# Gate rows through DRAM, join sums moved, weight loads reordered: one change to a fused spectral-filter and gated-MLP kernel

## Chip, cores, metric

One core of one Trainium2 chip. The metric is the device time of one execution in microseconds (us). A timed kernel is run several times, in turn with the kernel before on the same chip. A ratio is the mean time of one kernel's fast runs over the mean of the fast runs of the other in the same rounds, so it is not quite the ratio of the medians that are quoted. Faster or slower means by more than 2%. A profile is of one execution, taken by the hardware profiler: one of the timed ones, but for the kernel before, whose profile is of a further execution of 250.93 us. Its span is 1.7 to 2.0 us shorter than the timed figure of the same execution, so spans are compared with spans and medians with medians. Runs are marked slow (over 1.5% above the fastest of the same kernel); they stand in no ratio.

## The reference

```python
mod = (_silu(c) @ w_mod).reshape(1, 6, 1, 640)       # c: 1 x 640, w_mod: 640 x 3840
sa, ca, ga, sb, cb, gb = ...                         # six rows of 640
h = _layernorm(x) * (1 + ca) + sa                    # x: 1 x 2048 x 640
x = x + ga * irfft2(rfft2(h) * (w_r + 1j * w_i))     # spectral filter
h = _layernorm(x) * (1 + cb) + sb
x = x + gb * ((silu(h @ w_gate) * (h @ w_up)) @ w_down)   # w_gate: 640 x 1728
```

All tensors are bf16. Six modulation vectors are needed. `ca`, `sa`, `cb`, `sb` are used as columns (one value per partition). `ga` and `gb` are used as rows, the same row on all 128 partitions: `ga` multiplies the table `RI` of the last transform, `gb` multiplies the down weights.

## The kernel before, where the change touches it

The kernel runs in stages. **Stage 1** (to 35.8 us) makes layer norm 1 and the forward transform over the 640 columns. The **middle stage** takes spectral columns in groups: TensorE transforms a group (`stage_a`), VectorE multiplies by the filter (`prod`, two products per group, over the filter `Wn` and its flipped copy `Wv`), TensorE transforms back (`stage_b`, `stage_c`), and VectorE or GpSimd fill in the rotated halves (`rot`). At the **changeover** the first tiles of the last transform start (`s1em`, `s1er`). The **last spectral stage** makes 16 tiles of x1; layer norm 2 (LN2) of its first tiles, with a DMA transpose, is made beside it. Then come the **gate/up** and down products, continuous TensorE work to the end.

`Wn` and `Wv` each have three planes: real, imaginary and a "join sum" of both, made in pieces by `wsum` on VectorE or GpSimd.

```python
# SyncE's queue, early: gate-a weights (800 KB) ahead of Wv
nc.sync.dma_start(wm_r[:, :, 0, :], wm_m[:, :, 0, :])
nc.sync.dma_start(KS2, K_dram[:, 384:576])
# ... (cut)
for i in range(2):
    nc.sync.dma_start(Wv[:, 2 * i, :, :], Wflip[i][:])
# ... stage 1 (cut); then four DMA transposes in a row, and what follows them
t2_dma(0); t2_dma(1); t2_dma(2); t2_dma(3)
nc.sync.dma_start(wm_r[:, :, 1:3, :], wm_m[:, :, 1:3, :])   # LN2's weights, 1600 KB
nc.sync.dma_start(wm_r[:, :, 3, :], wm_m[:, :, 3, :])       # gate-b weights, 800 KB
nc.sync.dma_start(Htab[:], H_dram)
nc.sync.dma_start(RI[:], RI_dram)
# ... (cut: down weights, 2 x 960 KB and small pieces)
load_gu(0, 512)              # first gate/up block, 2 x 640 KB
load_gu(512, 1024, (0,))     # gate half of the second block, ahead of LN2's transpose

def mod_bc(j, lo, bank, o=0, ks=range(NC5)):     # half a gate row on all partitions: 5 products of 320 columns
    gps_ = psum[:, bank, o:o + 320]
    for k in ks:
        nc.tensor.matmul(gps_, lhsT=sc_rep[:, k, :], rhs=wm_r[:, k, j, lo:lo + 320], start=(k == 0), stop=(k == NC5 - 1))
    return gps_

# stage_a of the last four groups: LN2's columns, 50 one-column products in all
# ... (cut)
prod(g, PP, xps, 0)
if g == 0:
    wsum(Wv, 48, 64, nc.vector)        # join sum, between the first two products
prod(g, PP, xps, 1)

# ... changeover (cut)
nc.scalar.copy(gb_bc[:, 320:640], mod_bc(3, 320, 3, 128))
s1em(0)
s1em(1)
for q0, q1 in ((0, 8), (8, 32), (32, 64)):
    rot(64, 16, slice(q0, q1), nc.vector)
nc.vector.tensor_tensor(RI[:, 0], RI[:, 0], ga_bc[:], ALU.mult)
# ... last spectral stage, tile 4 (cut)
ln2_tr(0)                              # DMA transpose of LN2's first chunk
load_gu(512, 1024, (1,))
load_gu(1024, 1664)
```

## Time and profile before

| | before |
|---|---|
| median, 3 runs | 251.51 us (251.18 to 251.62) |
| span of the profile, granted clock | 249.1 us, 0.998 |
| end of stage 1 to first product of the changeover | 26.88 us (35.80 to 62.68) |
| changeover: that to the first output product | 2.07 us (to 64.75) |
| last spectral stage: that to the first gate/up product | 17.63 us (to 82.38) |
| gate/up to the end | 166.72 us |

The last four rows come from the timeline of TensorE: "end of stage 1" is the start of its last product there, the others are the starts of the first product of the line concerned. They add up to the span with the end of stage 1, so a difference between two kernels can be read off stage by stage. The prediction below shows the profile's own lines.

### The profile page before, as it was taken

How to read it: one execution, taken by the hardware profiler on the slowest of the kernel's cores; microseconds unless marked ns; L12 is line 12 of the kernel's file. 1: busy time of each engine (PE TensorE's matmuls, PEld its weight loads, DVE VectorE, ACT ScalarE, POOL GpSimd, SP SyncE). 2: the span in 40 equal slices, each digit the busy share in tenths (PEclk: the TensorE clock that was granted, in tenths of full speed). 3: DMA queues.
4: the chain of work that ended last, by engine and by line, in shares of the span. 5: the costliest groups of instructions: out<-in, count | busy, mean ns of one | idle time of the engine just before them, and what ended most of it. 6: DMA issues, size and time to landing. Idle time of an engine off the chain costs nothing.

```text
span 249.1 us, 6473 instructions
## 1 busy us (share of the span) xinstructions
PE 243.5 (98%) x2512; PEld 200.4 (80%) x2512; DVE 209.7 (84%) x524; ACT 162.7 (65%) x300; POOL 74.3 (30%) x122
## 2 busy tenths in 40 slices
PE   8999999999999999999999999999999999999994
PEld 3778877999889888688877778886768887779973
DVE  4798888998898997879997997879995888895895
ACT  3778666997788798488862487674356766235740
POOL 8487755894025422000003900001330000440000
PEclk9999999999999999999999999999999999999999
DMA  7999999999999999300005020003311000211001
GB/s 221 396 357 334 309 365 191 175 397 381 286 352 288 275 264 186 81 9 0 3 0 108 13 68 29 3 3 58 73 42 39 3 0 3 54 53 57 3 0 53
DMA packets 45760, 34.43 MB, mean 138 GB/s; under 512 B 21731, under 2 KB 42658, under 8 KB 45346
## 3 DMA queue, kind: packets, MB, share of 16 engines
q1 hardware_dynamic: 43936, 30.00, 42.8%
q0 software_dynamic: 1504, 3.95, 6.7%
q8 instruction: 19, 0.31, 0.5%
q10 hardware_dynamic: 290, 0.08, 0.1%
q14 instruction: 11, 0.09, 0.1%
HBM read 26.72 MB, written 4.72 MB: 126 GB/s over the span
## 4 chain that ended last, share of the span: by engine, by line
PE 80%; SPq 9%; DMA 6%; ACT 1%; DVE 1%; issue 1%; DVEq 0%; ACTq 0%
PE psum L1016 33%; PE psum L899 19%; PE psum L986 9%; DMA rW<-wflip_r 4%; PE psum L879 3%; PE psum L597 3%; PE psum L664 3%; PE psum L567 2%; SPq L273 2%; SPq L277 2%; PE psum L1149 2%; DMA rM<-in_w_mod_dram 2%; SPq L275 2%; PE psum L1152 2%; PE psum L974 2%; PE psum L618 2%
## 5 line engine op out<-in xcount | busy, mean ns | idle before, releaser
L1016 PEld LDWEIGHTS <-rW 128*128 128x128 bf16 (+1 forms) x528 | 46.9, 98 | 5.6 <-issue 0.2
L1016 PE MATMUL psum<-rW 128*128 128x256 bf16 (+1 forms) x240 | 27.1, 259 | 0.0
L913 POOL TENSOR_TENSOR rM<-rM,rL 128x320 f32<-128x320 f32 x6 | 5.9, 975 | 68.2 <-ACT rL L912 68.2
L899 PEld LDWEIGHTS <-rE 128*128 128x128 f16 (+1 forms) x196 | 19.1, 97 | 7.7
L1016 PE MATMUL psum<-rY,rW 128*128 128x256 bf16 (+1 forms) x96 | 24.0, 259 | 0.0
L986 PE MATMUL psum<-rW 128*128 128x256 bf16 (+1 forms) x170 | 23.1, 291 | 0.0
L899 PE MATMUL psum<-rE 128*128 128x320 f16 (+1 forms) x147 | 22.3, 299 | 0.0
L590 DVE TENSOR_TENSOR rM<-psum,rW 128x384 bf16<-128x384 f32 (+2 forms) x42 | 20.1, 541 | 2.0 <-PE psum L567 1.4
L986 PEld LDWEIGHTS <-rW 128*128 128x128 bf16 x170 | 16.6, 98 | 3.8
L1016 PEld LDWEIGHTS <-rE 128*128 128x128 f16 x192 | 17.4, 98 | 2.4
L899 PEld LDWEIGHTS <-rX 128*128 128x128 bf16 (+1 forms) x151 | 14.6, 97 | 5.4
L760 POOL TENSOR_TENSOR rstd<-rstd,mhalf 128x4 f32<-128x4 f32 (+2 forms) x4 | 4.5, 1120 | 48.2 <-DVE rstd L756 48.2
L1052 DVE TENSOR_TENSOR rH<-psum,rW 128x512 bf16<-128x512 f32 x21 | 14.5, 689 | 4.9 <-PE psum L1016 3.1
L1048 ACT COPY rH<-psum 128x512 f32<-128x512 f32 x21 | 12.3, 585 | 9.0 <-PE psum L1016 7.3
L1042 ACT COPY rW<-psum 128x512 f32<-128x512 f32 x21 | 12.3, 585 | 6.8 <-PE psum L1016 6.7
L1055 ACT COPY rX<-psum 128x512 f32<-128x512 f32 x21 | 12.3, 586 | 6.7 <-PE psum L1016 6.7
L1070 DVE TENSOR_TENSOR rX<-rH,rL 128x512 bf16<-128x512 bf16 x21 | 8.9, 423 | 9.1 <-ACT rL L1068 9.0
L382 DVE SCALAR_TENSOR_TENSOR rE<-rE,mv,psum 128x648 bf16<-128x648 f32 (+1 forms) x17 | 14.2, 844 | 2.1 <-PE psum L318 1.5
L1056 DVE TENSOR_TENSOR rX<-psum,rX 128x512 f32<-128x512 f32 x21 | 14.4, 685 | 1.7 <-ACT rX L1055 1.6
L899 PE MATMUL psum<-rA,rX 128*128 128x320 bf16 (+1 forms) x98 | 15.6, 299 | 0.0
L1016 PE MATMUL psum<-rH,rW 128*128 128x256 f16 (+1 forms) x96 | 15.1, 259 | 0.1
L1016 PE MATMUL psum<-rE,rY 128*128 128x256 f16 (+1 forms) x96 | 15.1, 259 | 0.0
(198 smaller groups left out, 674.3 us busy)
## 6 DMA issues: line engine op xcount, KB each, us to landing
out_dram<-rA SPq DMA_DIRECT2D x31, 80.0 KB, 1.6
rM<-in_w_mod_dram SPq DMA_DIRECT2D x3, 800.0 KB, 9.9
rX<-in_A_x_dram SPq DMA_DIRECT2D x3, 640.0 KB, 7.3
rA<-in_B_w_down_dram SPq DMA_DIRECT2D x2, 960.0 KB, 14.4
rM<-in_w_mod_dram SPq DMA_DIRECT2D x1, 1600.0 KB, 7.1
rY<-in_B_w_gate_dram POOLq DMA_DIRECT2D x2, 768.0 KB, 7.7
rW<-in_B_w_gate_dram SPq DMA_DIRECT2D x2, 640.0 KB, 7.2
rW<-in_B_w_up_dram SPq DMA_DIRECT2D x2, 640.0 KB, 6.5
```

The costliest lines, as they stand in the source:

```text
L382: nc.vector.scalar_tensor_tensor(Zv[:, h], Cv[:, h], mv[:, t, 0:1], zps[:, h], ALU.mult, ALU.subtract)
L590: nc.vector.tensor_tensor(PP[:, :, hl], xv[:, :, hl], in1, ALU.mult)
L597: nc.tensor.matmul(yps[:, i, :], lhsT=_rev(PP, 64 * n * ps + i, [[n, 128]]), rhs=identb[:], start=(ps == 1 and i == 0), stop=(ps == 0 and ...
L899: nc.tensor.matmul(o, lhsT=lhsT, rhs=rhs, start=start, stop=stop, skip_group_check=True)
L986: nc.tensor.matmul(gu[u], lhsT=Wgu[:, u, c5, ff * 128:(ff + 1) * 128], rhs=h2T[:, :, c5, :], start=(c5 == 0), stop=(c5 == NC5 - 1))
L1016: nc.tensor.matmul(o[:, f], lhsT=w, rhs=b, start=(start and f == 0 and i == 0), stop=(stop and f == F - 1 and i == len(ops) - 1), skip_gro ...
L1042: nc.scalar.copy(c0, X)
L1048: nc.scalar.copy(c2, X)
L1052: nc.vector.tensor_tensor(c11, Z, c0, ALU.add)
L1055: nc.scalar.copy(c3, X)
L1056: nc.vector.tensor_tensor(c22, Y, c3, ALU.add)
L1070: nc.vector.tensor_tensor(ato, v4(c11), v4(g21), ALU.mult)
```

## The change

Intent: take 2.7 us of 320-column products off TensorE by making `ga` and `gb` as columns (25 one-column products each), turning them into rows by one transposing product, a write to DRAM and a broadcasting read; bring Wv forward by putting gate a's weights behind it, with the join sum into a gap of VectorE ahead of the first product; take LN2's columns out of the middle stage and make them at the changeover; bring gate b's weights early, between the second and the third DMA transpose, because its columns are now made in the middle stage. Cut to its core:

```diff
-    nc.sync.dma_start(wm_r[:, :, 0, :], wm_m[:, :, 0, :])
     nc.sync.dma_start(KS2, K_dram[:, 384:576])
 ...
         nc.sync.dma_start(Ktab[:, 0:384], K_dram[:, 0:384])
+        nc.sync.dma_start(wm_ga[:], wm_m[:, :, 0, :])
 ...
         t2_dma(1)
+        nc.sync.dma_start(wm_r[:, :, 2, :], wm_m[:, :, 3, :])
         t2_dma(2)
         t2_dma(3)
-        nc.sync.dma_start(wm_r[:, :, 1:3, :], wm_m[:, :, 1:3, :])
-        nc.sync.dma_start(wm_r[:, :, 3, :], wm_m[:, :, 3, :])
-        nc.sync.dma_start(Htab[:], H_dram)
-        nc.sync.dma_start(RI[:], RI_dram)
 ...  (stage_a)
+                    for c5 in range(NC5) if g == 10 else ():
+                        mod_col(psum[:, b, 200 + c5:201 + c5], wm_r[:, :, 2], c5)
+                    if g in (7, 12):
+                        nc.tensor.matmul(g_ps(b), lhsT=gcol[:, int(g > 7), :], rhs=identb[:], start=True, stop=True)
             prod(g, PP, xps, 0)
-            if g == 0:
-                wsum(Wv, 48, 64, nc.vector)
             prod(g, PP, xps, 1)
+            if g == 10:
+                nc.vector.tensor_copy(gcol[:, 1], psum[:, b, 200:205])
+            if g in (7, 12):
+                nc.vector.tensor_copy(gT[:, int(g > 7)], g_ps(b))
+            if g == 7:
+                g_write(0, nc.sync)
+                nc.sync.dma_start(RI[:], RI_dram)
+                nc.sync.dma_start(Htab[:], H_dram)
+                g_row(0, nc.sync, ga_bc)
+                nc.sync.dma_start(wm_r[:, :, 0:2, :], wm_m[:, :, 1:3, :])
 ...  (middle stage and changeover)
         t2_pe(0)
+        wsum(Wv, 48, 64, nc.vector)
 ...
+            if g == 3:
+                for c5 in range(NC5):
+                    mod_col(psum[:, 6, c5:c5 + 1], wm_ga, c5)
+                nc.vector.tensor_copy(gcol[:, 0], psum[:, 6, 0:NC5])
 ...
+            if g == 12:
+                g_write(1, nc.gpsimd)
+            if g == NG - 5:
+                ri_fold(nc.gpsimd, slice(1, 2))
 ...
+        for t in range(2):
+            s1em(t)
+            if t == 0:
+                b_cols(0)
+        g_row(1, nc.gpsimd, gb_bc)
 ...
+        VTs = {0: s1er(0)}
+        b_cols(1)
+        VTs[1] = s1er(1)
```

Cut away: other pieces of the join sums moved between VectorE and GpSimd, the tiles of `s1em` two ahead instead of one, other PSUM banks, one of the two rotations of columns 40 to 47 moved from GpSimd to VectorE, and a cast of `sc_rep` on GpSimd that fell away.

## The prediction

> **What bounds the kernel now.** I read the page first, then the chain that ended last in order of time, then the engines' timelines from 35 to 65 us, where every edited line runs, and last the table of stretches. The page says TensorE is busy 98% of the span at full clock, and the chain says it is the limit nearly everywhere after the start.
>
> ```profile
> PE 243.5 (98%) x2512; PEld 200.4 (80%) x2512; DVE 209.7 (84%) x524; ACT 162.7 (65%) x300; POOL 74.3 (30%) x122
> PE 80%; SPq 9%; DMA 6%; ACT 1%; DVE 1%; issue 1%; DVEq 0%; ACTq 0%
> ```
>
> So work taken off TensorE counts, but only where the chain passes through TensorE. The chain in order of time shows where it does not (start, length, what):
>
> ```profile
> 18.69 4.65 SPq L277
> 23.38 3.89 SPq L279
> 27.32 1.08 SPq L280
> ...
> 29.07 9.58 DMA rW<-wflip_r
> 38.74 0.44 DVE rW L407
> 39.24 0.44 issue
> 39.68 1.02 DVE rM L590 x2
> 40.75 0.49 PE psum L567 x4
> ```
>
> Up to 38.65 us the end is set by the load of the flipped filter (Wv), and that load sits in SyncE's queue behind 800 KB of gate weights (line 279), whose issue alone held the queue 3.89 us. VectorE then does the join sum over Wv (line 407) and only after it the second product of the first group (line 590). From 40.75 on TensorE leads. The timeline of VectorE at this point:
>
> ```profile
> 36.89 0.49 DVE L542 TENSOR_TENSOR rM<-psum,gb_bc 128x256 bf16<-128x256 bf16 x2 [0.49 <-ACT rA L400]
> 37.81 0.56 DVE L590 TENSOR_TENSOR rM<-psum,rW 128x384 bf16<-128x384 f32 x1 [0.43 <-PE psum L567]
> 38.74 0.43 DVE L407 TENSOR_TENSOR rW<-rW 128x512 bf16<-128x512 bf16 x1 [0.37 <-DMA rW<-wflip_r]
> 39.21 4.52 DVE L590 TENSOR_TENSOR rM<-psum,rW 128x384 bf16<-128x384 f32 x10
> ```
>
> VectorE idles 0.43 us (to 37.81), idles 0.37 us for the DMA, and spends 0.43 us on the join sum; then come ten products back to back, one per 0.452 us. So the first 4.5 us of the middle stage (products, inverse transforms; 39 to 62 us) are bound by VectorE, the rest by TensorE.
>
> TensorE at the changeover to the last spectral stage:
>
> ```profile
> 62.00 0.84 PE L651 MATMUL psum<-rM,sc_rep 128*128 128x320 bf16 x5
> 62.68 1.14 PE L664 MATMUL psum<-rH,rE 128*128 128x128 bf16 x16
> 63.65 0.39 PE L669 MATMUL psum<-rH,rE 128*128 128x128 bf16 x4
> 63.87 0.84 PE L651 MATMUL psum<-rM,sc_rep 128*128 128x320 bf16 x5
> 64.75 0.31 PE L1149 MATMUL psum<-rH,rL 128*128 128x320 bf16 x1
> ```
>
> **What the skill says.** (1) "TensorE: Matmul & The Clock Gate", section Back-to-back issue gap: a matmul with one moving column costs the issue floor of about 25 ns, one with N columns about N/2.4 ns plus 2.5. The trace agrees: the chain has ten one-column products of line 571 in 0.23 us, 23 ns each, and five 320-column products of line 651 in 0.68 us, 136 ns each. The same section's 81 ns for a weight load and matmul pair at 128 columns is not what runs here: eight of line 597 take 0.45 us, 56 ns each. I use the trace. (2) "DMA: Bandwidth & Descriptors", section Queues, rings and completion order: on each DMA engine the descriptors of one queue are consumed in ring order. So moving 800 KB from before Wv to after it should bring Wv forward by the time of those bytes; the trace agrees so far as DMA share is 1.05 in 20 to 40 us. (3) Same page, Anatomy of one DMA: a fixed cost of about 2 us per DMA. The smallest DMA landings here (80 KB stores, 1.6 us) fit, so the DRAM round trip of a gate row is two such costs plus queueing, and must be hidden. (4) "SBUF — State Buffer", section SBUF: two separate sides: VectorE with two SBUF inputs and GpSimd exclude each other. The join sum of 512 elements took 0.425 us on VectorE but 1.154 on GpSimd; the page's lock itself is not shown by a trace of before.
>
> **The change, part by part.**
>
> *Gate rows.* Removed: four half rows, each five 320-column products, 4 x 0.68 = 2.7 us of TensorE; three casts on ScalarE and one of 0.49 us on VectorE; the 0.71 us cast of sc_rep on GpSimd (at 3.4 us, followed by a wait of GpSimd for a table, so worth nothing). Added: 2 x 25 one-column products, 2 x 25 x 23 ns = 1.15 us, and two 128-column transposing products, 2 x 0.056 = 0.11 us. TensorE's balance is -1.45 us. By place it is less: the two half rows of ga ran at 35.9 to 39.35, while VectorE and the DMA led, so their 1.36 us are worth little there. The two of gb ran at 62 to 64.7 on the chain, 1.36 us. All of the added 1.26 us lands in the middle stage where TensorE leads.
>
> *LN2 columns late.* The 50 one-column products of line 571 (50 x 23 ns = 1.15 us) leave the middle stage and come back at its end, as 25 after the first half of the final stage's first tile and 25 a little later. So the middle stage has +1.26 - 1.15 = +0.1 us of TensorE; the changeover has -1.36 + 1.15 = -0.2.
>
> *Queue order.* wm_ga is 819 KB. At the 309 to 365 GB/s of the slices from 25 to 37 us that is 2.2 to 2.7 us, so Wv should land at about 38.65 - 2.4 = 36.2 us. The join sum now stands between the line 542 adds and the first product: it starts at 37.38 and ends at 37.81, just when the first product started before. Then the second product starts at 38.3 and not 39.21: **-0.9 us** for the VectorE-bound row of products. The moved sums before it (512 and 1024 elements after the last tile, 0.42 + 0.68 = 1.1 us in place of 0.95) end at about 36.6, before the adds at 36.89, so cost nothing. The first DMA transpose landed at 41.34 and the same bytes are still ahead of it, so group 5 can run at 41.6 on GpSimd's add, and its products were at 42.6 before: an advance of 0.9 just fits. I take -0.8.
>
> *Changeover, 62.16 to 64.75, 2.59 us.* After: 0.45 + 0.58 + 0.45 + 0.11 + 0.58 + 0.11 = 2.28 us of TensorE. But VectorE is nearly as late: from the last ScalarE eviction (63.12) it does the rotations, 1.04, a copy 0.15, and the first half fold of RI, about 0.28 (a whole one is 0.48), to 64.6; the other fold went to GpSimd. So -0.15 rather than -0.3.
>
> *Final spectral stage, 64.75 to 82.54.* 15 full tiles of output products at 0.55, 14 of s1 at 0.56 and gu13's 0.55 make 16.6 between the first tile and the last, against 17.24 measured: 0.6 us of gaps, at tiles 2 to 4 where LN2 fills VectorE, and at evictions of VT by ScalarE. With s1 two tiles ahead, the VT waits go, the VectorE waits stay: -0.2.
>
> Sum: -0.8 + 0.1 - 0.15 - 0.2 = -1.05; the rest, from 82.5 on, is continuous TensorE work that only shifts. 251.5 - 1.05 = about **250.4 us**.
>
> **Rivals.** *A, GpSimd becomes the bound at the end of the middle stage.* It gets one join sum more (1.15), a fold of 640 elements (estimate 1.15 x 640/512 = 1.44), and the DRAM write's descriptors (0.5 to 0.8, as its other DMA issues took), and loses one rotation (0.62): +2.6 us. It had idle time of 1.02 us at 41.3, and 1.30 and 2.08 late:
>
> ```profile
> 58.57 1.20 POOL L646 TENSOR_SCALAR rE<-rE 128x512 bf16<-128x512 bf16 x2 [1.30 <-ACT rE L635]
> 61.85 0.62 POOL L646 TENSOR_SCALAR rE<-rE 128x512 bf16<-128x512 bf16 x1 [2.08 <-DVE rE L635]
> ```
>
> It should just fit, as the last rotation's wait is no longer its own. If the third transpose, now 2.5 us behind the gb weights, lands late, GpSimd stands still for it at its add at about 49 us and the rotations end after TensorE wants them: +0.5 to +1, so 251 to 251.4. *B, Wv does not land before 37.4.* Then the join sum holds up both first products, the start gains at most 0.4 and the total is 251.0. Against it: 2.4 us of bytes are gone before it, and 1.2 are needed. *C, TensorE's gaps close.* From 35.8 to 64.75 it had about 26.2 us of work in 28.95; if the whole -1.45 shows and the start gap closes, the time is 249.4. Against it: VectorE has 19.8 of 21.4 us busy in the middle stage, so it holds TensorE. *D, the DRAM round trip or the LN2 weights come late.* ga is written at about 47 us and wanted by the fold at 56; LN2's weights are now behind that round trip on SyncE's queue, wanted at 61.5, and I expect them at 58 or 59. A stall would cost 1 to 2 us; unlikely.
>
> **Range and chances.** A weighs about a quarter, B and D a tenth each, C a fifth. From 249.5 (C) to 251.2 (A and B) should hold it 8 times in 10. 2% is 5 us; the whole TensorE balance is 1.45 us, so faster by 2% is about 0.01. Slower by 2% needs a stall of 5 us in a queue, 0.01.
>
> **What would show it.** The Wv load landing at 36 to 37; the join sum at about 37.4 and no wait for wflip_r on VectorE; the second product of line 590 near 38.3; the first output product about 1 us before 64.75; 0.1 to 0.3 us less between it and the gate/up stage; TensorE's busy time down by about 1 us or more, and the span by the same. Wrong if: VectorE still waits for wflip_r; TensorE's s1 products wait for GpSimd's rotations; a wait for wm_r, ga_bc or RI appears near 57 to 62 us.

## The result

| | before | after |
|---|---|---|
| median | 251.56 us (251.18 to 251.82), 4 runs | 255.32 us (253.92 to 255.86), 4 runs |
| ratio of fast runs | | 1.0142, 95% interval 1.0099 to 1.0185 |
| span, granted clock | 249.1, 0.998 | 253.8, 0.992 |
| end of stage 1 | 35.80 | 36.54 |
| middle stage, to the changeover | 26.88 | 25.55 |
| changeover | 2.07 | 4.84 |
| last spectral stage | 17.63 | 19.35 |
| gate/up to the end | 166.72 | 167.52 |

So the kernel became 1.4% slower, inside the 2% of "same", but 4.9 us above the predicted time and 4.1 us above the top of the range. By stage, after minus before is +0.74 - 1.33 + 2.77 + 1.72 + 0.80 = 4.70 us, the difference of the spans. The line between middle stage and changeover isn't drawn at the same work in both kernels: before, the first half row of gate b (line 651, 0.68 us, from 62.00 on) stands ahead of it, after, nothing does. The prediction counts that half row with the changeover. Drawn so, the middle stage is 26.20 us before and 25.55 after (-0.65), the changeover 2.75 and 4.84 (+2.09).

Two of these five terms aren't the change's. The 0.74 at the end of stage 1 is scatter of the first loads: the other kernels below that contain the same start end stage 1 between 35.6 and 36.1. The 0.80 after the start of gate/up is two-valued over all runs: apart from two kernels treated below, that stretch is either 166.6 to 166.9 or 167.4 to 167.7 us, and versions of the kernel before land in both. The other three make 3.16 us; the means of the fast runs differ by 3.6. The page of the changed kernel, engines' busy time and chain by engine:

```profile
PE 245.1 (97%) x2544; PEld 200.9 (79%) x2544; DVE 211.6 (83%) x527; ACT 161.8 (64%) x298; POOL 75.6 (30%) x124
PE 71%; DMA 13%; DVE 7%; POOL 3%; ACT 2%; SPq 2%; issue 1%; DVEq 0%; ACTq 0%; POOLq 0%
```

TensorE was to be less busy by a microsecond, and is busier by 1.6, though work was taken from it. And DMA has 13% of the chain in place of 6%, while the early chain over Wv is gone. First the part that worked, VectorE at the start of the middle stage (start, length, line, what):

```profile
37.62 0.49 DVE L546 TENSOR_TENSOR rM<-psum,gb_bc 128x256 bf16<-128x256 bf16 x2 [0.41 <-ACT rA L402]
38.02 0.42 DVE L409 TENSOR_TENSOR rW<-rW 128x512 bf16<-128x512 bf16 x1
38.54 3.81 DVE L610 TENSOR_TENSOR rM<-psum,rW 128x384 bf16<-128x384 f32 x8
```

The join sum (line 409) now stands in the gap ahead of the first product and waits for no load; the products follow without a break. The second one starts some 0.45 us after the first, at 38.99, which is 2.45 us after the end of stage 1, against 3.41 before: 0.96 us earlier. Now the chain of the changed kernel in order of time:

```profile
42.25 5.67 DMA rM<-in_w_mod_dram
47.97 0.78 PE psum L567 x25
...
50.31 2.07 DMA ga_d<-gT
52.76 11.65 DMA rM<-in_w_mod_dram
64.46 0.78 PE psum L567 x25
65.24 0.81 PE psum L675 x8
...
75.41 7.46 DMA rW<-rL
83.62 1.85 POOL rW L816 x3
85.52 0.38 PE psum L1004 x2
```

Three loads stand in it that weren't there before. The gate-b weights (42.25) land just after their columns want them (TensorE waits 0.35 us). Then four issues stand ahead of LN2's weights on SyncE's queue (start, time in which the issue held the queue):

```profile
50.31 0.52 SPq L530 DMA_DIRECT2D ga_d<-gT  x1
50.88 0.37 SPq L595 DMA_DIRECT2D rH<-tab_RI  x1
51.31 0.41 SPq L596 DMA_DIRECT2D rH<-tab_H  x1
52.40 0.32 SPq L533 DMA_DIRECT2D ga_bc<-ga_d  x1
52.76 0.68 SPq L598 DMA_DIRECT2D rM<-in_w_mod_dram  x1
```

Of the 2.07 us of gate a's write to DRAM, SyncE issues RI and H in the first part and stands still only in the last 0.6 us, ahead of the read of the row (line 533). LN2's weights are issued at 52.76, and not at 47.30 as before, and land at 64.41, 11.65 us later. And LN2's transpose (75.41) takes 7.46 us, so that GpSimd's modulation of its result (line 816) ends after TensorE wants it. Both waits are on TensorE's timeline:

```profile
62.64 0.55 PE L675 MATMUL psum<-rH,rE 128*128 128x128 bf16 x7 [0.33 <-DVE rE L666]
64.46 0.78 PE L567 MATMUL psum<-sc_col,rM 128*128 128x1 bf16 x25 [1.27 <-DMA rM<-in_w_mod_dram]
67.46 0.47 PE L1177 MATMUL psum<-rH,rL 128*128 128x320 bf16 x1
69.41 0.30 PE L1177 MATMUL psum<-rH,rL 128*128 128x320 bf16 x1
85.52 0.38 PE L1004 MATMUL psum<-rW,Wp 128*128 128x256 bf16 x2 [0.50 <-POOL rW L816]
```

1.27 us of waiting is only part of the 2.77. The third and fourth lines are the same product, and the span of the third is half as long again: after the wait TensorE runs at half speed (granted clock 0.50 from 66 to 68 us). The chain gives the same for eight 128-column products of line 675, 0.81 us at 65.24 against 0.45 from 69 us on.

### The profile page after: what moved, and what is told of

It reads as the page before. It is cut to its first block, busy times and chain, and to the rows that moved or that the text cites. A ratio compares the mean times of both kernels' runs of the same rounds, so it can differ in the third digit from the quotient of the medians.

```text
span 253.8 us, 6555 instructions
## 1 busy us (share of the span) xinstructions
PE 245.1 (97%) x2544; PEld 200.9 (79%) x2544; DVE 211.6 (83%) x527; ACT 161.8 (64%) x298; POOL 75.6 (30%) x124
## 2 busy tenths in 40 slices
DMA packets 45995, 34.78 MB, mean 137 GB/s; under 512 B 21805, under 2 KB 42860, under 8 KB 45580
## 4 chain that ended last, share of the span: by engine, by line
PE 71%; DMA 13%; DVE 7%; POOL 3%; ACT 2%; SPq 2%; issue 1%; DVEq 0%; ACTq 0%; POOLq 0%
PE psum L1046 31%; PE psum L929 13%; DMA rM<-in_w_mod_dram 9%; PE psum L1016 9%; PE psum L909 3%; DMA rW<-rL 3%; PE psum L675 1%; PE psum L320 1%; PE psum L317 1%; PE psum L395 1%; SPq L519 1%; PE psum L337 1%; PE psum L396 1%; PE psum L1004 1%; PE psum L362 1%
## 5 line engine op out<-in xcount | busy, mean ns | idle before, releaser
L790 POOL TENSOR_TENSOR rstd<-rstd,mhalf 128x4 f32<-128x4 f32 (+2 forms) x4 | 4.8, 1194 | 49.4 <-DVE rstd L786 49.4
L1182 DVE SCALAR_TENSOR_TENSOR rM<-psum,rX 128x640 f32<-128x640 f32 x16 | 13.1, 821 | 3.5 <-PE psum L1180 3.4
```

The costliest lines, as they stand in the source:

```text
L1182: nc.vector.scalar_tensor_tensor(x1[:, t, :].rearrange("p (m r) -> p m r", r=4), ops.rearrange("p r m -> p m r"), 1.0, x_sb[:, t, :].rearr ...
```

## The experiments

The expectations name theories by letter. The main ones: **F**, that the DMA queues have no slack from the start of the middle stage to gate/up, so that a load put ahead of another makes that one late, and what counts is which load lands after its user wants it; **E**, that the early start of two loads on GpSimd's queue (the fallen cast) shifts the first loads; **Q**, that the order on SyncE's queue made the loss; **G**, in the first texts that GpSimd and the gate arithmetic made it, and in that of start_edit_alone that the start edit spoils the transposes. Three groups follow: what the waits cost, which move makes them, and whether repaired versions keep the gain. The reader can judge each by the stage columns in the table at the end of this section.

### What the waits cost

**ln2_first**: LN2's weights ahead of the write of gate a's row, so they don't wait for the DRAM write.

```diff
             if g == 7:
+                nc.sync.dma_start(wm_r[:, :, 0:2, :], wm_m[:, :, 1:3, :])
                 g_write(0, nc.sync)
                 ...
                 g_row(0, nc.sync, ga_bc)
-                nc.sync.dma_start(wm_r[:, :, 0:2, :], wm_m[:, :, 1:3, :])
```

> Changed kernel with one move: the load of the LN2 weights (1600 KB) is issued before the write of the ga row, so it no longer stands behind that write's DRAM round trip and behind the 1344 KB of RI and Htab. Theory Q (the queue order made the loss): the load lands near 57 us instead of 64.4, TensorE's wait of 1.3 us before the LN2 columns goes, the granted clock stays at 1.0 from 60 to 70 us (0.83 in the changed kernel), the first output product comes at about 64.7 instead of 66.9, and the time falls from 255.1 to 252 to 253. Rival G (GpSimd and the gate arithmetic made the loss): the load lands early too, but the first half of the final stage still starts late because the rotations on GpSimd end late, and the time stays over 254.

255.08 us (254.08 to 256.68; a fourth run, 257.91, was slow), ratio 1.0136 (1.0077 to 1.0196). The wait for LN2's weights is gone, and no time with it. GpSimd's timeline, and TensorE's:

```profile
61.81 1.40 POOL L694 TENSOR_TENSOR rH<-rH,ga_bc 128x640 bf16<-128x640 bf16 x1 [3.53 <-DMA ga_bc<-ga_d]
64.48 0.56 PE L675 MATMUL psum<-rH,rE 128*128 128x128 bf16 x7 [2.72 <-POOL rE L666]
```

Now gate a's row (160 KB) is behind the 1.6 MB and lands at 61.7. GpSimd's fold waits 3.53 us for it, the rotations behind the fold are late, and TensorE waits 2.72 us for them. One wait took the other's place: both loads can't be first.

**fold_last**: ln2_first, with GpSimd's fold behind all rotations.

```diff
-            if g == NG - 5:
-                ri_fold(nc.gpsimd, slice(1, 2))
 ...
             rot(l0, n, slice(0, 64), nc.gpsimd, (i,))
+        ri_fold(nc.gpsimd, slice(1, 2))
```

> As ln2_first (LN2 weights ahead of the ga row's round trip), and the fold of the ga row into RI moved behind all rotations on GpSimd. In ln2_first the fold waited 3.53 us for the ga row (until 61.81) and the last two rotations stood behind it, so TensorE waited 2.7 us for GpSimd. Theory Q+G (two waits in turn: SyncE's queue, then GpSimd's order): the wait of TensorE for the rotations goes to under 0.4 us, the first output product comes at 64.5 to 65 instead of 67.4, the clock of 60 to 70 us stays at 1.0, and the time is 252 to 253. Rival (the loss lies elsewhere): over 254.

254.88 us (254.09 to 255.25), ratio 1.0124 (1.0098 to 1.0150). The changeover shrinks from 5.88 (ln2_first) to 3.11 us, so the rotations behind the fold were the cause there. But the row still lands at 64.4, and LN2's transpose takes 8.22 us; the last spectral stage is 20.11.

**warm_wait**: six 512-column products on ones, without use, ahead of LN2's first columns, so TensorE isn't idle while it waits.

```diff
             if t == 0:
+                idle_pe(6)
                 b_cols(0)
```

> Changed kernel with six 512-column dummy products ([...]1.3 us) put before the first LN2 column products, where TensorE otherwise sits idle for the LN2 weights. Nothing arrives sooner. If the half speed of TensorE from 65.1 to 68.8 us comes of that idle time, the 320-column products stay at 0.14 us each instead of 0.27, and the first two output tiles come 1.0 to 1.2 us sooner after the weights land: 254 to 254.5. If the clock is unrelated to the wait, the granted clock of 60 to 70 us stays near 0.83 and the time stays at 255 or is longer.

254.99 us (253.26 to 256.58), ratio 1.0123 (1.0056 to 1.0191); the timing can't tell it from the change. The trace can: granted clock 1.00 from 60 to 70 us against 0.83 after, LN2's columns to the first output product 1.93 us (64.04 to 65.97) against 2.47, and the last spectral stage 0.52 shorter. So the half speed after the wait cost about 0.54 + 0.52 = 1.06 us of the loss. Not every wait is paid so. In the other traces the clock fell after waits of 1.38 us (rows_on_act_less_ahead, 48.3 us), 1.56, 2.58, 2.72, 3.75, 4.87 and 7.69 us, but stayed at 1.00 after those of 1.10 us and less, and also after 1.66 us in gate_b_late (94.4 us) and 1.34 us in products_quiet_queue (95.3 us). What decides isn't shown.

**late_edges**: the change with the fallen cast of GpSimd put back. **before_early_edges**: the kernel before with that cast moved behind the two early loads. (Theory E.)

```diff
+        nc.gpsimd.tensor_copy(rL.cut(0, [NC5, 128]), sc_f[:].unsqueeze(2).to_broadcast([P, NC5, 128]))   # late_edges
         flip_edge(A_w_i, Wflip[0])
         flip_edge(A_w_r, Wflip[1])
```

```diff
-        nc.gpsimd.tensor_copy(sc_rep[:], sc_f[:].unsqueeze(2).to_broadcast([P, NC5, 128]))   # before_early_edges
         flip_edge(A_w_i, Wflip[0])
         flip_edge(A_w_r, Wflip[1])
+        nc.gpsimd.tensor_copy(sc_rep[:], sc_f[:].unsqueeze(2).to_broadcast([P, NC5, 128]))
```

> Changed kernel with a dummy cast of 640 elements put back on GpSimd ahead of the four small DRAM-to-DRAM copies of the flip edges, as the removed cast of sc_rep stood there. Theory E (these copies, now issued 1.2 us sooner, collide with the first loads and delay the first table by 0.85 us): the table lands at about 4.8 us again, the first stage ends at 35.8 and not 36.5 us, and the time falls by 0.7 us, to 254.4. Rival (the late first loads are scatter between executions): no change of the first stage that goes with the edit.

> Kernel before with the cast of sc_rep moved behind the four small copies, so that they are issued 1.2 us sooner, nothing else. Theory E: the first stage ends 0.7 us later and the time grows from 251.5 to about 252.2. Rival (scatter): 251.5, unchanged.

255.3 us (253.48 to 255.93), ratio 1.0125 (1.0074 to 1.0176), and 251.6 us (251.5 to 251.83), ratio 0.9989 (0.9952 to 1.0026). Stage 1 ends at 35.91 and 35.97. Theory E falls: the 0.74 us of the first trace isn't from the early loads.

### Which move makes the waits

**before_gb_between**: the kernel before with one line moved: gate b's weights between the second and third transposes.

```diff
         t2_dma(1)
+        nc.sync.dma_start(wm_r[:, :, 3, :], wm_m[:, :, 3, :])
         t2_dma(2)
 ...
-        nc.sync.dma_start(wm_r[:, :, 3, :], wm_m[:, :, 3, :])
```

> Kernel before with one move: the load of the gb weights (800 KB) issued between the second and the third transpose, as the changed kernel has it. Theory F: the third and fourth transposes land 2.4 us later (800 KB at some 340 GB/s), the add of the third on GpSimd (at 49.3) and the group that needs it (group 13) wait up to 1 us: 251.8 to 252.6. Rival: transposes have slack, no change (251.5).

256.86 us (256.59 to 257.01), ratio 1.0190 (1.0161 to 1.0220). This single move costs at least as much as the whole change (1.0142, 1.0099 to 1.0185). SyncE's queue in the kernel before, then in this one (start, time in which the issue held the queue):

```profile
36.76 6.94 SPq L519 DMA_TRANSPOSE rL<-rA  x3
43.81 3.44 SPq L519 DMA_TRANSPOSE rM<-rA  x1
47.30 0.59 SPq L527 DMA_DIRECT2D rM<-in_w_mod_dram  x1
```

```profile
41.51 0.75 SPq L525 DMA_DIRECT2D rM<-in_w_mod_dram  x1
42.31 4.87 SPq L519 DMA_TRANSPOSE rL<-rA  x1
47.28 3.79 SPq L519 DMA_TRANSPOSE rM<-rA  x1
51.12 0.58 SPq L528 DMA_DIRECT2D rM<-in_w_mod_dram  x1
```

The load itself holds the queue 0.75 us, but the third transpose behind it holds it 4.87 us, where before it held it 2.02 (41.68 to 43.70). That its issue is held while the 800 KB ahead are moved fits this, but what it waits for isn't shown. LN2's weights are issued at 51.12 in place of 47.30. In the kernel before they landed at about 54.4 (47.30 plus the 7.1 us that the DMA view gives) and were first used at 54.76: a slack of about 0.4 us. Here TensorE's timeline has

```profile
59.13 0.40 PE L571 MATMUL psum<-sc_col,rM 128*128 128x1 bf16 x10 [3.75 <-DMA rM<-in_w_mod_dram]
```

and after it a granted clock of 0.59 from 60 to 63 and 0.84 from 63 to 66 us. The wait and the lost clock, 3.75 + 3 x 0.41 + 3 x 0.16, make 5.5 of the 5.8 us by which the middle stage is longer. So with the early gate-b weights LN2's columns couldn't stay where they were; these parts of the change belong together. It also shows the limit: whatever moved ahead of LN2's weights took its time from 0.4 us of slack.

**before_row_copies**: the kernel before with four broadcasting copies of 160 KB into scratch, two behind RI on SyncE and two on GpSimd, to measure what the rows' traffic costs.

```diff
         nc.sync.dma_start(RI[:], RI_dram)
+        for _ in range(2):
+            nc.sync.dma_start(rY.cut(6144, [D]), <row of c on all partitions>)
 ...
+        for _ in range(2):
+            nc.gpsimd.dma_start(rY.cut(6144, [D]), <row of c on all partitions>)
         s1em(0)
```

> Kernel before with four extra copies of one DRAM row to all partitions (160 KB each) into scratch that nothing reads: two on SyncE's queue behind RI, two on GpSimd's queue at the end of the middle stage. Twice the row traffic of the change, no round trip, nothing waits for it. Theory F: the LN2 transpose lands 1.5 to 2 us later relative to its issue, and as it had 1.1 us to spare the time grows by 0.4 to 1 us. Rival (row copies are free, the waiting is what costs): 251.5, unchanged.

258.49 us (256.8 to 259.75; a fourth run, 262.64, was slow), ratio 1.0250 (1.0187 to 1.0313). The experiment was badly built: all copies write the same scratch, so each waits for the one before, and SyncE's queue stood 12.27 us at this line. It doesn't measure 160 KB of traffic. What it does show is that a wait on SyncE's own queue, as the change has a short one for gate a's write, makes all later loads late: the last spectral stage took 24.43 us in place of 17.63.

**start_edit_alone**: the kernel before with only the start of the change: gate a's weights behind Wv, the moved join sums, gate a's half rows as before but at group 3.

```diff
-    nc.sync.dma_start(wm_r[:, :, 0, :], wm_m[:, :, 0, :])
 ...
         nc.sync.dma_start(Ktab[:, 0:384], K_dram[:, 0:384])
+        nc.sync.dma_start(wm_r[:, :, 0, :], wm_m[:, :, 0, :])
 ...
-        ga_mod(320, 5, range(3))
         t2_pe(0)
+        wsum(Wv, 48, 64, nc.vector)
 ...
+            if g == 3:
+                ga_mod(0, 6)
+                ga_mod(320, 7)
```

> The kernel before with only the part of the change at the start: gate-a weights loaded behind Wv, join sums in the new places, the two half rows of gate a as 320-column products in the middle stage (at the place where the change has its one-column products). Transposes, LN2 weights, tables, gate-b row as before. Theory F: the second product stands 0.95 us earlier against the end of stage 1, the rows' 1.36 us come onto TensorE's path in the middle stage, the 800 KB move from ahead of the transposes to beside their start. Sum 251.5 - 0.95 + 1.36 = 251.9, range 251.2 to 252.6. Rival G (the moved gate-a load itself disturbs the transposes and costs the two microseconds that rows_on_pe still shows): 253.5 or more, with a transpose landing over 1 us later than in before.

251.75 us (251.55 to 251.87) against 252.19 of before in the same rounds, ratio 0.9978 (0.9945 to 1.0011). Middle stage 26.85 against 26.88, everything else unchanged. Theory G falls: the start edit harms nothing. It also gains nothing so, since its 0.95 us are paid back by gate a's ten 320-column products, 1.36 us, which before had run under a wait. They were free there, and aren't here.

**before_less_ahead**: the kernel before with the 640 KB gate load of the second block behind LN2's transpose.

```diff
-    load_gu(512, 1024, (0,))
 ...
                 ln2_tr(0)
-                load_gu(512, 1024, (1,))
+                load_gu(512, 1024)
```

> The kernel before with one edit: the 640 KB gate load of the second column block, issued at 67.66 us of the before trace, is issued behind the LN2 transpose instead. Same edit that took rows_on_act from 254.32 to 252.44 us. Theory F (the DMA queue decides, and what counts is which load lands after its user wants it): the transpose of before already lands at about 77.8 us, before its data are wanted, so nothing is gained here: 251.5 us, ratio to before 0.998 to 1.003. Rival (less traffic ahead of the transpose helps any kernel, so the gain of rows_on_act_less_ahead says nothing on the change): 249.8 us, ratio about 0.993.

252.01 us (251.78 to 252.21) against 252.19, ratio 0.9986 (0.9947 to 1.0026). No gain: before, the transpose comes in time anyway.

### Repaired versions

**rows_on_act**: gate a's row written and read on ScalarE's queue, after groups 7 and 11, so that SyncE waits for nothing; LN2's weights, RI and H straight behind the transposes' issue at group 7.

```diff
             if g == 7:
-                g_write(0, nc.sync)
-                ...
+                nc.sync.dma_start(wm_r[:, :, 0:2, :], wm_m[:, :, 1:3, :])
+                nc.sync.dma_start(RI[:], RI_dram)
+                nc.sync.dma_start(Htab[:], H_dram)
 ...
+            if g == 7:
+                g_write(0, nc.scalar)
+            if g == 11:
+                g_row(0, nc.scalar, ga_bc)
```

> Changed kernel with the ga row's write and read-back issued from ScalarE's queue (after groups 7 and 11) instead of SyncE's, and the LN2 weights issued before RI and H. SyncE then waits for no DRAM write, and the small copies do not stand behind 1.6 MB on one ring. Theory Q: the ga row lands before 56 us, GpSimd's fold waits for nothing, the LN2 weights land near 57, no wait of TensorE before either, first output product at 64.5 to 65; time 251.5 to 252.5, the rest of the loss being the wait of 0.5 us for the gb weights at 47.5. Rival (the DMA engines are simply full): the LN2 weights or the H table still land after 62 and the time stays above 253.5.

254.32 us (253.09 to 256.21), ratio 1.0131 (1.0084 to 1.0177). The LN2 wait is gone, the clock is 1.00, and the first output product stands 28.90 us after the end of stage 1 (30.39 in the change, 28.95 before). The loss up to there is repaired in this trace; that in the last spectral stage (19.59) isn't. The trace is of the fastest of the four runs, and the ratio can't be told from that of the change. The edit moves two things at once, the row to another queue and LN2's weights ahead of RI and H. The chain has

```profile
72.84 8.23 DMA rW<-rL
```

for LN2's transpose, which before took 5.79 us (71.83 to 77.62).

**rows_on_act_gb_later**: the same, with gate b's columns two groups later.

```diff
-                    for c5 in range(NC5) if g == 10 else ():
+                    for c5 in range(NC5) if g == 12 else ():
```

> As rows_on_act, and the gb columns taken in group 12 instead of 10, transposed in group 14. The gb weights land at about 47.9 us, when TensorE had already waited for them 0.35 to 0.7 us in all runs so far; two groups later (some 2 us) that wait is gone. Expected 0.3 to 0.6 us less than rows_on_act: 251 to 252. If the wait was hidden anyway by VectorE, no difference.

254.54 us (254.0 to 256.44), ratio 1.0128 (1.0085 to 1.0171). The wait for gate b's weights went, and a wait of 1.6 us for the H table came, with a clock of 0.83 after it.

**rows_on_act_less_ahead**: rows_on_act, with the 640 KB load behind LN2's transpose (the diff of before_less_ahead).

> As rows_on_act, where the first output product came at 64.96 (0.2 us later than before) and yet gate/up began at 84.55 (2.2 us later), because the LN2 transpose issued at 72.84 took 8.2 us to land (6.0 before). Here one weight load of 640 KB (gate, columns 512 to 1024) is issued after that transpose and not ahead of it. Theory F (the DMA engines are full and serve in order, so the transpose waits for the backlog before it): it lands within 6.5 us, gate/up starts near 83, time 1.3 to 1.8 us under rows_on_act, about 252.7. Rival (the transpose itself or its producers are slow): still 8 us, no gain.

252.44 us (252.35, 252.37, 252.52, and one of 255.03) against 252.01, ratio 1.0041 (0.9986 to 1.0096): 1.9 us better than rows_on_act, and not told apart from the kernel before. The profile fell on the run of 255.03, so it can't show where the others gained. It shows what that run lost: gate a's row landed at 62.2 us, GpSimd's fold waited 1.72 us for it, and gate b's weights were waited for 1.38 us, with half speed after it.

**rows_by_products**: the rest of the change, with the gate rows by 320-column products as before, no DRAM trip.

```diff
-                for c5 in range(NC5):
-                    mod_col(psum[:, 6, c5:c5 + 1], wm_ga, c5)
+                for h in range(2):
+                    nc.scalar.copy(ga_bc[:, 320 * h:320 * h + 320], mod_bc(wm_ga, 320 * h, 6 + h))
 ...
-        g_row(1, nc.gpsimd, gb_bc)
+        nc.vector.tensor_copy(gb_bc[:, 0:320], mod_bc(wm_r[:, :, 2], 0, 5))
```

> The gate rows by 320-column broadcast products again as in the kernel before (ga in the middle stage, gb at its end), no DRAM trip; everything else as changed: ga weights behind Wv, gb weights between the transposes, LN2 columns late, the join sums moved. TensorE has 1.5 us more work than in the changed kernel. If the DRAM trip and what waits for it made the loss, this runs in 251 to 252 us although it has more TensorE work. If the order of the weights between the transposes or the late LN2 columns made it, it stays at 254 or more.

253.06 us (252.58 to 253.86), ratio 1.0059 (1.0030 to 1.0087): the best of those that keep the gate-b weights between the transposes and the 640 KB ahead. The last spectral stage is 17.61 us as before. What stays is the third transpose, on TensorE's timeline

```profile
51.74 0.50 PE L589 MATMUL psum<-Ktab,rL 128*128 128x192 bf16 x4 [0.79 <-POOL rL L566]
```

(it was on its way from 43.09 to 51.34, and GpSimd waited 1.09 us for it), and a changeover of 4.26 us, where TensorE waits 0.92 us for VectorE's copy of LN2's columns.

**products_quiet_queue**: that, with gate b's weights behind the tables and the 640 KB load behind LN2's transpose.

```diff
         t2_dma(1)
-        nc.sync.dma_start(wm_r[:, :, 2, :], wm_m[:, :, 3, :])
         t2_dma(2)
 ...
         nc.sync.dma_start(Htab[:], H_dram)
+        nc.sync.dma_start(wm_r[:, :, 2, :], wm_m[:, :, 3, :])
```

> rows_by_products (253.06 us) with its gate-b weights moved from between the transposes to behind the tables, and the 640 KB gate load behind the LN2 transpose. No row copies, no DRAM round trip, four transposes back to back. Theory F: the wait of TensorE for the third transpose (0.8 us) goes, the LN2 weights land by 57, the first output product stands at 65.5 or before, 251.5 us, range 250.8 to 252.2. Rival: what rows_by_products lost was the VectorE modcols beside the rotations, and it stays at 252.8 or more.

254.74 us (254.5 to 256.04), ratio 1.0108 (1.0066 to 1.0150): worse. The middle stage improves to 26.93, but gate b's weights, 12.1 us on their way, are now waited for at its end (1.1 us), VectorE's copy still holds TensorE 0.92 us, and gate/up waits 1.3 us for the deferred load.

**rows_on_pe**: the gate rows broadcast by TensorE (a gate column as a weight broadcast over 128 columns, times the unit matrix), transposes back to back, no DRAM trip.

```diff
+    nc.tensor.matmul(psum[:, bank, o + 128 * j:o + 128 * j + 128],
+                     lhsT=gcol[:, i, c + j:c + j + 1].to_broadcast([P, 128]), rhs=identb[:], start=True, stop=True)
```

> A version meant to beat both: from the changed kernel, gate rows as one-column products, but spread over the partitions by TensorE (each column repeated 128 times as the stationary operand, times the identity: five 128-column products, 0.28 us a row) and no DRAM trip; ga at groups 6 and 7 where TensorE had waited 0.7 us for an eviction; gb after the second and fourth output tiles; the four transposes back to back as before, then LN2 weights, RI, H, gb weights. Theory Q+F: no wait of TensorE for weights, rotations or H, the transpose of LN2 on time; first product of the stage 0.9 us earlier as in the changed kernel; 250.3 to 251.3. If it stays above 252, something else of the change costs.

254.69 us (254.0 to 256.08), ratio 1.0124 (1.0079 to 1.0168). No load is waited for by TensorE up to the first output product, but at 45.9 us gate a's columns wait 1.10 us until ScalarE has emptied their bank of PSUM (the memory that products are written to), at 48.9 TensorE waits 0.94 us for ScalarE's added copy, and gate b's columns wait 0.92 us for a bank that VectorE empties in the last spectral stage, which is 19.79.

**rows_in_order**: the rows through DRAM on ScalarE's queue, and behind four transposes in a row RI, H, gate b's weights, LN2's weights; gate b's columns at group 12; the 640 KB late.

```diff
         t2_dma(3)
+        nc.sync.dma_start(RI[:], RI_dram)
+        nc.sync.dma_start(Htab[:], H_dram)
+        nc.sync.dma_start(wm_r[:, :, 2, :], wm_m[:, :, 3, :])
+        nc.sync.dma_start(wm_r[:, :, 0:2, :], wm_m[:, :, 1:3, :])
```

> The change with its rows still going through DRAM, but nothing of the queue out of order: four transposes back to back, then RI, H, gate-b weights, LN2 weights; row writes and reads of gate a on ScalarE's queue; gate-b columns two groups later; the 640 KB gate load behind the LN2 transpose. Theory F: no wait on a DMA above 0.3 us from 40 to 66 us, granted clock 1.0 in 60 to 70, first output product at 64.2 or before, 251.2 us, range 250.5 to 252.2. Rival (the row copies alone, 160 KB each, still cost 1 us or more by filling the queues): 252.5 or more, with the LN2 weights or the LN2 transpose landing late though nothing was put ahead of them.

260.56 us (259.55 to 260.94), ratio 1.0322 (1.0281 to 1.0363). My expectation had a slip: group 12's columns are wanted at 49.4 us, when the weights have only just been issued. They land at 57.0 and TensorE waits 7.69 us. It shows why the change brought those weights in between the transposes, as long as gate b's columns stand in the middle stage.

**gate_b_late**: gate b is used first at 77.7 us, by the folds of the down weights, so its columns can go to the changeover. The order behind the transposes is LN2's weights, RI, H, gate b's weights; gate a's row is written after group 5 and read after group 9 on ScalarE's queue; gate b's row goes through DRAM at tiles 2 and 5, and the folds are two tiles later; the 640 KB late. **gate_b_late_gu_early**: the same with the 640 KB load where it was.

```diff
         t2_dma(3)
+        nc.sync.dma_start(wm_r[:, :, 0:2, :], wm_m[:, :, 1:3, :])
+        nc.sync.dma_start(RI[:], RI_dram)
+        nc.sync.dma_start(Htab[:], H_dram)
+        nc.sync.dma_start(wm_r[:, :, 2, :], wm_m[:, :, 3, :])
 ...
         b_cols(1)
+        for c5 in range(NC5):
+            mod_col(psum[:, 7, 200 + c5:201 + c5], wm_r[:, :, 2], c5)
 ...
-            if t >= 7 and t % 2:
-                wd_fold((t - 7) // 2)
+            if t in (9, 11, 12, 13, 15):
+                wd_fold((9, 11, 12, 13, 15).index(t))
```

> The change with gate b's columns taken out of the middle stage (gate b is first used in the folds of the down weights at 77.7 us, so nothing forces its weights in at 48): four transposes back to back, then LN2 weights, RI, H, gate-b weights, as before had them but for the order of the last three; gate-a row written after group 5 and read after group 9 on ScalarE's queue; gate-b columns beside the second LN2 columns at the changeover, its row written and read at tiles 2 and 5; the down-weight folds two tiles later; 640 KB gate load behind the LN2 transpose. Theory F: no wait on a DMA over 0.3 us from 40 to 66 us, middle stage 25.3 us from the end of stage 1 (26.88 before), changeover about 3.0 (2.07 before), last spectral stage 17.7 (17.63 before), 250.6 us, range 250.0 to 252.0. Rival (the row copies' 160 KB alone cost 1 us or more wherever they stand, or VectorE with the moved folds becomes the bound of the last spectral stage): 252.3 or more, with a row landing late or with the last spectral stage over 18.5.

> gate_b_late with the 640 KB gate load ahead of the LN2 transpose, as in the change. Theory F: the queue is now as full as in before at that place (the first gate/up load issued at about 63 to 64), so the transpose lands about 6.5 us after its issue and the gate/up stage waits 0 to 0.8 us: 250.6 to 251.6 us. If it costs 1.5 us or more over gate_b_late, what counts is the 640 KB themselves, not the place of the gate-b weights.

253.64 us (253.47, 253.64 and 255.07; a fourth run, 261.68, was slow), ratio 1.0095 (1.0058 to 1.0133), and 254.76 us (254.39 to 256.38), ratio 1.0139 (1.0096 to 1.0183). The whole times miss the expectations by 3 to 4, but the stages say where. The middle stage is 25.02 us (25.3 expected), the changeover 3.08 (3.0), TensorE waits for no load up to there, and the clock is 1.00: the first output product stands 28.10 us after stage 1, 0.85 earlier than before. This is the gain that was predicted. It's gone again by the end: in the last spectral stage (19.00 us) the row of gate b holds VectorE's folds 1.2 us, and TensorE loses about 0.7 us around VectorE's copy of the transposed gate-b column. And in gate/up, TensorE's timeline has

```profile
83.01 9.69 PE L1011 MATMUL psum<-rW 128*128 128x256 bf16 x85
94.36 5.09 PE L1011 MATMUL psum<-rW 128*128 128x256 bf16 x45 [1.66 <-DMA rW<-in_B_w_up_dram]
```

a wait of 1.66 us for the up weights behind the deferred load. With the 640 KB back in their place (gate_b_late_gu_early) that wait is gone, and the last spectral stage is 22.37 us, with VectorE held 3.2 us by gate b's row and LN2's transpose late: GpSimd starts on it 9.8 us after its issue, 6.0 before.

### All runs by stage

Spans and stages from the profiles in us; "first output" is the time from the end of stage 1 to the first output product, middle stage and changeover together. In the kernels whose name begins with before, in start_edit_alone, rows_by_products and products_quiet_queue the middle stage includes gate b's half row of 0.68 us, in the others it doesn't; "first output" is free of this. The ratio is the timed one.

| kernel | middle | changeover | first output | last spectral | gate/up to end | ratio |
|---|---|---|---|---|---|---|
| before | 26.88 | 2.07 | 28.95 | 17.63 | 166.72 | 1 |
| before_early_edges | 26.86 | 2.08 | 28.94 | 17.62 | 167.57 | 0.9989 |
| before_less_ahead | 27.15 | 2.08 | 29.23 | 17.62 | 167.63 | 0.9986 |
| start_edit_alone | 26.85 | 2.08 | 28.93 | 17.62 | 167.57 | 0.9978 |
| before_gb_between | 32.70 | 2.08 | 34.78 | 17.62 | 166.88 | 1.0190 |
| before_row_copies | 27.56 | 2.08 | 29.64 | 24.43 | 166.66 | 1.0250 |
| after | 25.55 | 4.84 | 30.39 | 19.35 | 167.52 | 1.0142 |
| late_edges | 26.39 | 4.09 | 30.48 | 20.05 | 167.46 | 1.0125 |
| ln2_first | 25.74 | 5.88 | 31.62 | 18.06 | 166.82 | 1.0136 |
| fold_last | 27.09 | 3.11 | 30.20 | 20.11 | 166.67 | 1.0124 |
| warm_wait | 25.98 | 4.17 | 30.15 | 18.83 | 166.70 | 1.0123 |
| rows_on_act | 26.15 | 2.75 | 28.90 | 19.59 | 166.65 | 1.0131 |
| rows_on_act_gb_later | 27.71 | 2.92 | 30.63 | 19.62 | 166.62 | 1.0128 |
| rows_by_products | 27.35 | 4.26 | 31.61 | 17.61 | 166.85 | 1.0059 |
| products_quiet_queue | 26.93 | 4.13 | 31.06 | 17.60 | 168.36 | 1.0108 |
| rows_on_pe | 27.35 | 2.45 | 29.80 | 19.79 | 166.80 | 1.0124 |
| rows_in_order | 34.83 | 2.51 | 37.34 | 17.58 | 166.78 | 1.0322 |
| gate_b_late | 25.02 | 3.08 | 28.10 | 19.00 | 168.80 | 1.0095 |
| gate_b_late_gu_early | 25.03 | 3.08 | 28.11 | 22.37 | 166.67 | 1.0139 |

(rows_on_act_less_ahead is left out, as its profile is of a run 2.5 us slower than its other three.) No version is faster than the kernel before; those that can't be told from it are before_early_edges, before_less_ahead, start_edit_alone and rows_on_act_less_ahead.

## Why the prediction was wrong, step by step

**The start** was right. It said -0.9 us for the second product, and counted 0.8 of it; the trace shows 0.96 earlier, no wait for Wv (its first half landed at 33.85 us in place of 35.75), and the join sum in its gap. (The DMA share of 1.05 that the prediction gives as agreement shows full engines, not an order; the earlier landing is what agrees.) start_edit_alone shows the same start by itself, and that it is worth only what else stays out of the middle stage.

**The middle stage** was right: -0.8 + 0.1 = -0.7 was predicted and -0.65 measured, with the half row counted as the prediction counts it. This includes a wait of 0.35 us for gate b's weights, which was not foreseen. gate_b_late, with gate b's columns out as well, has -1.18 by the same count.

**The changeover** was wrong: -0.15 predicted, +2.09 measured. The step that failed is rival D, "LN2's weights are now behind that round trip on SyncE's queue, wanted at 61.5, and I expect them at 58 or 59. A stall would cost 1 to 2 us; unlikely". They landed at 64.41. Their issue is 5.46 us later than before. 0.74 of this is the later end of stage 1; 2.2 is the transposes, with the 800 KB between them (the fourth ends 13.67 us after stage 1 in place of 11.45; before_gb_between shows this alone); 2.5 is what now stands between the fourth transpose and the load: the write, RI, H and the row, with the 0.6 us in which SyncE waits for the write. And the 1.6 MB took 11.65 us from issue to landing in place of 7.1. With RI, H and the row behind them they took 8.7 (ln2_first) and 8.8 (rows_on_act), so about 2.9 of the longer way go with what was issued ahead of them. The round trip itself was mis-sized too: the prediction put it at two costs of about 2 us plus queueing. Gate a's write took 2.07 us and its row 7.0, gate b's, on GpSimd's queue, 7.2 and 6.2. Of the +2.09, 1.27 are the wait for LN2's weights, 0.33 a wait for rotations, and 0.54 the half clock until the first output product, as warm_wait shows. That leaves -0.05 for the work itself, so no large term is missing.

**The last spectral stage** was wrong: -0.2 predicted, +1.72 measured. Here a step was missing altogether. The prediction took everything from 82.5 us on as "continuous TensorE work that only shifts", and never asked when LN2's transpose would land. It is issued as the first tiles end, 3.6 us later than before, and took 7.46 us in place of 5.79; GpSimd's modulation hangs on it, and TensorE's five products of line 1004 on that: 1.76 us from their first to the next output product, in place of 0.55. That is 1.2 of the 1.72; the other 0.52 is the half clock again. A part of the change that the prediction booked as a gain, the tiles of `s1em` two ahead, works against this. One more tile of it (0.56 us) stands ahead of the tiles that LN2 needs, and the transpose is issued 7.9 us or more after the first output product in every kernel with it, 7.1 in every kernel without (but for before_row_copies). Before, the modulation ended 1.0 us ahead of these products (80.30 and 81.28), so these 0.8 us count. No run puts that part back alone; what it costs by itself isn't shown.

**Rival A** was named with the right place. In the change GpSimd's fold waited 0.71 us for gate a's row (3.53 in ln2_first), but TensorE's 0.33 us are a wait for rotations on VectorE, which had taken one over from GpSimd; TensorE waited for GpSimd's in ln2_first (2.72 us). **Rivals B and C** didn't happen.

**What carries the explanation.** That the order of the queue is the cause is shown by before_gb_between (one moved load, +4.9 us) and by rows_on_act, where the loss up to the first output product goes away, in the trace, when the row leaves SyncE's queue and LN2's weights go ahead of RI and H. That the clock's drop adds about 1 us is shown by the trace of warm_wait; its times can't tell it. That the intended gain is real up to the first output product is shown by gate_b_late (-0.85 us). That it survives nowhere to the end has been seen in all versions that were traced, mostly with another load that lands late, in rows_on_pe with waits for PSUM banks and copies. It isn't that no load can move: 800 KB in start_edit_alone and 640 KB in before_less_ahead moved at no cost that shows.

**What stays open.** The fast runs of one changed kernel differ by up to 3.3 us, those of before by less than 2 in the same rounds; why isn't known. That the 640 KB load behind LN2's transpose took 1.9 us off rows_on_act, while gate/up waited 1.3 and 1.66 us for the deferred load in two other kernels, was not resolved, since no profile of a fast run of rows_on_act_less_ahead exists. And what the 160 KB row copies cost by themselves was not measured, as before_row_copies measured a wait.

## What to carry to other kernels

Before moving a load, list every load behind it in the queue, with the time at which it lands and the time at which its first user wants it; the smallest of these differences, here 0.4 us, is what the move may cost, and a small queue wait for a store counts as a move of all that follows. A saving on the leading engine of one microsecond is worth less than one late load, all the more as a wait of that engine can be paid a second time in a lower clock, as 1.27 us at 64 us were here (1.66 us at 94 us were not). Where the whole time says only that a version is slower, a table of stages by the trace shows which part of the change did its work and where it was given back.

## What the Trainium skill lacked or had wrong

- "TensorE: Matmul & The Clock Gate", Part 1 (the clock gate), gives the slow clock to a TensorE that was idle for a whole window of about 3.4 us. Here a single wait of 1.27 us, with 0.33 us of another just before it, was followed by some 3.5 us at half speed (eight 128-column products in 0.81 us at 65.24, and again 0.45 from 69 us on; granted clock 0.83 from 60 to 70). With the wait filled by products the clock stayed at 1.00. A wait of 1.66 us at 94.4 us (gate_b_late) left it at 1.00, so the length of the wait alone doesn't tell.
- "DMA: Bandwidth & Descriptors", Anatomy of one DMA, fits about 2 us plus bytes over 436 GB/s, for DMAs of GpSimd's queue. Gate a's write of 1.2 KB, on SyncE's queue, agrees with it (2.07 us). With other loads ahead it says little: gate b's write of 1.2 KB, on GpSimd's queue, took 7.2; 1.6 MB, by the fit 5.8 us, took 7.1 in the kernel before and 11.65 after; 160 KB, by the fit 2.4 us, took 8.3 in gate_b_late. The page has no word on how to estimate a landing behind a filled queue, nor that the issue of a DMA transpose behind an 800 KB load held SyncE's queue for 4.87 us (2.02 without the load).
- "TensorE: Matmul & The Clock Gate", Back-to-back issue gap, gives 81 ns for a weight load and product at 128 columns; the traces read here have 56 ns (eight in 0.45 us), which the page gives for a product alone.
